# Attention over 32 inducing points and a rational feed-forward layer in one kernel: activation tables swapped per eight units instead of ten, the second layer's matmuls split around the first layer's

## The chip, the cores and the metric

The kernel runs on one core of a Trainium2 chip. The metric is device time in microseconds (us) from start to end of one execution; the time of the kernel before is the median of three runs. Engines are named as in the profile: PE (TensorE matmuls), PEld (its weight loads), DVE (VectorE), ACT (ScalarE), POOL (GpSimd) and SP, which issues the DMAs. Each engine works through its own queue in order, so an instruction that waits holds up everything behind it on that engine.

## The reference

Inputs are x (4 batches of 12480 tokens, 128 channels), 32 inducing rows, w_in (128 x 2048), w_out (2048 x 128) and six scalars a and b. x and the inducing rows are float32, w_in and w_out float64, which the kernel turns to float32 on the chip.

```
h    = softmax(inducing @ x.T / sqrt(128)) @ x        # 32 rows per batch
attn = softmax(x @ h.T / sqrt(128)) @ h               # 12480 rows per batch
h    = attn @ w_in                                    # 49920 x 2048
P    = a0 + a1 h + a2 h^2 + a3 h^3
Q    = 1 + |b0| |h| + |b1| h^2
out  = (P / (Q + 1e-6)) @ w_out                       # 49920 x 128
```

## The kernel before

Since attn is a weighted sum of 32 rows, the kernel multiplies these 32 rows by w_in once per batch (`piece`, tile `st`) and makes each hidden value from 32 softmax weights (tile `at`). Both are kept as high and low f16 parts, stacked on the partitions.

The work of the feed-forward layer is cut into 832 **units** (`main`, line 1044): 4 batches x 26 blocks of 480 tokens x 8 eighths of the hidden layer. A unit has 256 hidden columns, as two halves k = 0, 1 of 128 x 480 values. Its number within its block is q = 0..7. A unit passes through these steps, each on tiles of 960 columns:

- `first` (PE): two f16 matmuls into the PSUM tile `hp`, of which there are three.
- the absolute value u. Units with q = 0, 2, 4, 5, 6 get it as a bit mask on DVE (`mask`), followed by two more matmuls that add a constant to `hp` (`moved`, rows "hp<-same,by"); units with q = 1, 3, 7 have that constant in `st` and get it by an Abs on ACT.
- a product on DVE, `last.g` (rows "l<-u,all,hp"), after which `hp` is free.
- on ACT, for the pair of two units at once (1920 columns), Ln in place of u (rows "u<-u") and later Sigmoid in place of that (rows "u<-u,all"). Ln and Sigmoid lie in different activation tables, so the kernel gathers several pairs of one kind before it turns to the other.
- a second product: for even units on DVE (rows "l<-l,all,u"), for odd units on POOL in two instructions (`last_on_pool`, rows "u<-l,all" and "l<-u").
- `second` (PE): for each half k an f32 matmul by `w_out` into the PSUM tile `po` (there is one), accumulated over the eight units of a block. Each f32 matmul shows as two MATMUL rows, so a unit has four. After q = 7 two more matmuls (rows "po<-at,st") add a linear part. Then `fetch` copies `po` to `oT` on DVE (row "oT<-po") and issues the DMA of the block on SP.

`fast_ticks` (line 885) writes the order out by hand, tick by tick; the order on every engine is fixed to program order. In tick t the mask or Abs is that of unit t, the matmuls of `first` are those of unit t+1, `last.g` is that of unit t-1, the second product is that of units t-13 (DVE) and t-12 (POOL), in odd ticks, and `second` is that of unit t-14, called `done`. A tick whose `done` has q = 0 is `late`: there `second` comes after everything else of the tick, since it needs `po` empty.

Besides, `side` (line 782), called near the end of each tick, makes the attention of the coming blocks and batches in small steps, under a budget of DVE, POOL and PE time per tick. It begins with `self.fetch()`, ahead of its own steps. `second` sets `self.full` after q = 7; `fetch` does nothing while that is None and sets it back to None.

The softmax Exps of the attention wait in a list and are run by `run_act` once per group, in the tick with `turn == TURNS`, right before that group's first Sigmoid. They have a table load of their own.

With TURNS = 5, a group is ten units. Counted from the first unit of the group, the five Lns come in ticks 7 to 11, the five Sigmoids in ticks 12 to 16, and the DVE products in ticks 13, 15, 17, 19, 21.

Of the kernel before, what the change touches and what calls it, by code (L numbers as in the profile page):

```python
# [28 lines left out]
S16 = 2.0 ** 6  # L29
Z = A16 * S16  # L30
LIMIT = 900.0
TURNS = 5
BEHIND = 2 * TURNS + 3


def convert_weights(nc, pool, raw, dst, width, name, rooms):
# [156 lines left out]
class Kernel:  # L193
# [350 lines left out]
    def plain(self, t):  # L544
        return t if self.fast else t.bitcast(F32)
# [302 lines left out]
        for k in range(2):  # L848
            self.nc.tensor.matmul(u.h[:, k], self.by, self.same, start=False, stop=True, skip_group_check=True)

    def second(self, u):

        nc = self.nc
        b, n, q = u.key
        if q == 0:
            self.po = self.ps_o.tile([P, 512], F32, tag="po", name=f"po{u.i}")
        for k in range(2):
            fc = 2 * q + k
            nc.tensor.matmul(self.po[:, 0:BT], self.w_out[:, fc, :], u.g[:, k], start=(fc == 0), stop=(fc == self.NF - 1 and not self.fast))
        if q == self.NP - 1 and self.fast:  # L860
            self.until(lambda: "linear" in self.ready_cols[b])
            for i in range(2):
                nc.tensor.matmul(self.po[:, 0:BT], self.lin[b][:, C * i:C * i + C], u.rhs, start=False, stop=(i == 1))
        if q == self.NP - 1:
            self.full = b, n, self.po
            self.ended = b * self.NB + n + 1
            if n == self.NB - 1:
                self.left = b
# [16 lines left out]
    def fast_ticks(self, units):  # L885

        V, A, p = self.nc.vector, self.nc.scalar, self.params  # L890
        n = len(units)
        at = lambda t: units[t] if 0 <= t < n else None
        plain = lambda u: not self.shifted(u.key[2])

        def mask(u):
            V.tensor_scalar(out=u.u.bitcast(I32), in0=u.h.bitcast(I32), scalar1=0x7FFFFFFF, scalar2=None, op0=ALU.bitwise_and)

        self.first(units[0])
        for t in range(n + BEHIND + 2):
            u, last, d, done = at(t), at(t - 1), at(t - BEHIND), at(t - BEHIND - 1)  # L900
            group, turn = divmod(t - TURNS - 2, 2 * TURNS)
            w = at(2 * TURNS * group + 2 * (turn % TURNS))
            late = done and done.key[2] == 0
            if late:
                self.fetched = self.fetch()
            if t % 2 and at(t + 1):
                self.first(at(t + 1))
            if done and not late:
                self.second(done)
            if t % 2 == 0 and at(t + 1):  # L910
                self.first(at(t + 1))
            if u:
                if t % 2 == 0:
                    u.pair = self.mp.tile([P, 2, 2, BT], F32, tag="u", name=f"u{u.i}", bufs=self.rooms["u"])
                    u.u = u.pair[:, 0]
                    mask(u)
                else:
                    u.u = last.pair[:, 1]
                    if not plain(u):
                        A.activation(u.u, u.h, AF.Abs, bias=p.z_back, scale=1.0)  # L920
            if t % 2 and d:
                V.scalar_tensor_tensor(out=d.g, in0=d.g, scalar=p.z_k3, in1=d.u, op0=ALU.add, op1=ALU.mult)
                self.last_on_pool(at(t - BEHIND + 1), d)
            if u and t % 2 and plain(u):
                mask(u)
            if last:
                last.g = self.new(last, "l")
                V.scalar_tensor_tensor(out=last.g, in0=last.u, scalar=p.z_k1, in1=last.h, op0=ALU.add, op1=ALU.mult)
            if u and plain(u):
                self.moved(u)  # L930
            self.run_act(turn == TURNS)
            if w and turn < TURNS:
                A.activation(w.pair, w.pair, AF.Ln, bias=LAM, scale=LAM / Z)
            elif w:
                A.activation(w.pair, w.pair, AF.Sigmoid, bias=p.lnc, scale=-2.0)
            self.side(u or units[-1])
            if late:
                self.second(done)
        self.fetch()

# [155 lines left out]
```

## Time and profile before

| | us |
|---|---|
| median of 3 runs | 2682.53 (2680.53 to 2683.49) |
| the profiled execution | 2690.05 |
| its span, first to last instruction | 2688.2 |
| PE busy | 2408.0 (90%) |
| DVE busy | 2265.7 (84%) |
| ACT busy | 2099.1 (78%) |
| POOL busy | 1446.9 (54%) |

The first 115 us or so prepare weights and the first batch; the units' last `last.g` is on DVE at 2649 us, and the rest is the way out of the pipeline. Up to about 2100 us the attention's steps run beside the units, after that few are left. Engine names at the front of a row say who worked or waited; "<-" inside names reads "written from"; a bracket or a last column gives idle time ahead of the instruction and who ended it.

### The profile page before, as it was taken

How to read it: one execution, taken by the hardware profiler on the slowest of the kernel's cores; microseconds unless marked ns; L12 is line 12 of the kernel's file. 1: busy time of each engine (PE TensorE's matmuls, PEld its weight loads, DVE VectorE, ACT ScalarE, POOL GpSimd, SP SyncE). 2: the span in 40 equal slices, each digit the busy share in tenths (PEclk: the TensorE clock that was granted, in tenths of full speed). 3: DMA queues.
4: the chain of work that ended last, by engine and by line, in shares of the span. 5: the costliest groups of instructions: out<-in, count | busy, mean ns of one | idle time of the engine just before them, and what ended most of it. 6: DMA issues, size and time to landing. Idle time of an engine off the chain costs nothing.

```text
span 2688.2 us, 25782 instructions
## 1 busy us (share of the span) xinstructions
PE 2408.0 (90%) x8662; PEld 1217.6 (45%) x8662; DVE 2265.7 (84%) x2487; ACT 2099.1 (78%) x1445; POOL 1446.9 (54%) x997
## 2 busy tenths in 40 slices
PE   8589988999988988999999889999989899989997
PEld 5344544554534444554544334545444444444443
DVE  2687888879887997889888788889889899999995
ACT  1167788778777798888777788788878889889886
POOL 0234555555554555556555555556556565666566
PEclk8589999999999999999999999999999999999999
DMA  9112200220112200210212101211010100000000
GB/s 249 42 52 78 73 27 11 59 64 28 48 56 64 65 26 22 63 56 27 58 59 66 44 15 33 63 41 37 25 38 22 41 16 29 17 17 19 15 15 16
DMA packets 117111, 121.02 MB, mean 45 GB/s; under 512 B 13289, under 2 KB 115561, under 8 KB 116969
## 3 DMA queue, kind: packets, MB, share of 16 engines
q1 hardware_dynamic: 116969, 119.28, 15.6%
q8 instruction: 70, 1.15, 0.2%
q14 instruction: 72, 0.59, 0.1%
HBM read 80.89 MB, written 25.56 MB: 40 GB/s over the span
## 4 chain that ended last, share of the span: by engine, by line
PE 45%; DVE 25%; ACT 13%; issue 10%; POOL 2%; DMA 2%; SPq 1%; DVEq 0%; ACTq 0%; POOLq 0%
PE po L177 27%; DVE l L177 11%; DVE u L177 10%; PE hp L177 10%; ACT u L177 9%; ACT L177 3%; PE pd L177 3%; PE ph L177 2%; PE pc L177 1%; DVE oT L177 1%; DVE asm L177 1%; SPq L177 1%; POOL l L177 1%; PE pl L177 1%; POOL u L177 1%
## 5 line engine op out<-in xcount | busy, mean ns | idle before, releaser
L177 PE MATMUL po<-l,w_out 128*128 128x480 f32 x3328 | 1488.9, 581 | 25.8 <-DVE l L177 20.2
L177 DVE SCALAR_TENSOR_TENSOR l<-u,all,hp 128x960 f32<-128x960 f32 x832 | 1001.2, 1204 | 57.4 <-PE hp L177 57.2
L177 POOL TENSOR_SCALAR u<-l,all 128x960 f32<-128x960 f32 x416 | 446.4, 1073 | 1039.4 <-DVE l L177 934.4
L177 POOL TENSOR_TENSOR l<-u 128x960 f32<-128x960 f32 x416 | 928.3, 2231 | 34.6
L177 PEld LDWEIGHTS po<-l,w_out 128*128 128x128 f32 x3328 | 636.2, 194 | 581.0 <-issue 463.2
L177 ACT ACTIVATE u<-u,all 128x1920 f32<-128x1920 f32 x416 | 765.4, 1887 | 1.0
L177 ACT ACTIVATE u<-u 128x1920 f32<-128x1920 f32 x416 | 727.8, 1795 | 17.5 <-DVE l L177 16.5
L177 DVE TENSOR_SCALAR u<-hp 128x960 int32<-128x960 int32 x520 | 596.0, 1146 | 82.2 <-PE hp L177 77.1
L177 ACT ACTIVATE u<-hp,all 128x960 f32<-128x960 f32 x312 | 329.3, 1055 | 426.6 <-PE hp L177 407.5
L177 DVE SCALAR_TENSOR_TENSOR l<-l,all,u 128x960 f32<-128x960 f32 x416 | 519.0, 1248 | 129.8 <-ACT u L177 129.7
L177 PE MATMUL hp<-at,st 128*128 128x480 f16 x1664 | 483.4, 373 | 40.5 <-DVE l L177 36.4
L177 PE MATMUL hp<-same,by 96*128 96x480 f16 x1040 | 303.0, 373 | 146.9 <-DVE u L177 141.6
L177 PEld LDWEIGHTS <-st 128*128 128x128 f16 x1872 | 182.0, 100 | 419.8 <-issue 358.5
L177 ACT ACT_TABLE_LOAD x193 | 247.6, 1283 | 3.9 <-PEq L1089 0.7
L177 PEld LDWEIGHTS <-by 96*128 96x128 f16 x1040 | 102.5, 99 | 280.6 <-issue 181.7
L177 PEld LDWEIGHTS pd<-HT,xTb 128*120 128x120 f32 x832 | 103.0, 197 | 23.3 <-DMA xTb<-x_c 10.0
L177 DVE COPY oT<-po 128x480 f32<-128x480 f32 x104 | 67.7, 651 | 51.0 <-PE po L177 50.7
L177 PE MATMUL pd<-HT,xTb 128*120 128x32 f32 x832 | 100.1, 275 | 9.9 <-DMA xTb<-x_c 9.4
L177 PE MATMUL pc<-xTa,ind 128*128 128x480 f32 x156 | 74.1, 578 | 11.6 <-DMA xTa<-x_c 11.6
L177 PE MATMUL ph<-x,eT 120*32 120x129 f32 x624 | 78.2, 277 | 2.2 <-DMA x<-x_t 2.2
L177 PEld LDWEIGHTS ph<-x,eT 120*32 120x32 f32 x624 | 65.8, 111 | 23.7 <-issue 15.9
L177 PE MATMUL po<-at,st 128*128 128x480 f16 x208 | 59.1, 366 | 0.0
(108 smaller groups left out, 673.4 us busy)
## 6 DMA issues: line engine op xcount, KB each, us to landing
xTb<-x_c SPq DMA_DIRECT2D x104, 240.0 KB, 2.8
out<-oT SPq DMA_DIRECT2D x104, 240.0 KB, 2.0
xTa<-x_c SPq DMA_DIRECT2D x78, 240.0 KB, 2.8
x<-x_t SPq DMA_DIRECT2D x78, 240.0 KB, 3.3
at<-hl SPq DMA_DIRECT2D x416, 30.0 KB, 1.8
xw<-x_t SPq DMA_DIRECT2D x8, 720.0 KB, 14.8
xTw<-x_c SPq DMA_DIRECT2D x5, 960.0 KB, 10.1
raw<-w_in SPq DMA_DIRECT2D x4, 480.0 KB, 13.3
```

Source lines behind the costliest of these rows:

```text
L177: ins = call(*args, **kw)
```

## The change

Three things change in `fast_ticks` and `second`.

First, TURNS is 4 and BEHIND, which was 2 x TURNS + 3 = 13, is written as 13. A group is eight units: counted from its first unit, Lns in ticks 6 to 9, Sigmoids in ticks 10 to 13, DVE products in ticks 13, 15, 17, 19. The distance from a unit's mask to its second product stays 13 ticks. There are 104 groups instead of 84.

Second, in ticks that are not late PE's order is: half k = 0 of `second`, then `first` of unit t+1, then half k = 1 (with the linear part if q = 7). Before, `first` was ahead of both halves in odd ticks and behind both in even ticks.

Third, the call of `fetch` at the start of a late tick is put behind the mask of that tick, and where no unit is left, ahead of `second`.

```
-TURNS = 5
-BEHIND = 2 * TURNS + 3
+TURNS = 4
+BEHIND = 13
...
-    def second(self, u):
+    def second(self, u, ks=(0, 1)):
...
-        if q == 0:
+        if q == 0 and 0 in ks:
             self.po = self.ps_o.tile([P, 512], F32, tag="po", name=f"po{u.i}")
-        for k in range(2):
+        for k in ks:
...
+        if 1 not in ks:
+            return
...
-            if late:
-                self.fetched = self.fetch()
-            if t % 2 and at(t + 1):
+            if done and not late:
+                self.second(done, (0,))
+            if at(t + 1):
                 self.first(at(t + 1))
             if done and not late:
-                self.second(done)
-            if t % 2 == 0 and at(t + 1):
-                self.first(at(t + 1))
+                self.second(done, (1,))
             if u:
                 if t % 2 == 0:
...
                     mask(u)
+                    if late:
+                        self.fetched = self.fetch()
...
             self.side(u or units[-1])
             if late:
+                if not u:
+                    self.fetch()
                 self.second(done)
```

## Rows read from the trace of the kernel before

**Rows 1.** The page's chain of work that ended last, by engine.

```profile
PE 45%; DVE 25%; ACT 13%; issue 10%; POOL 2%; DMA 2%; SPq 1%; DVEq 0%; ACTq 0%; POOLq 0%
```

**Rows 2.** Busy time of each engine in two stretches: a middle one, with attention beside the units, and the last one before the pipeline empties. Columns: stretch, length, busy us (instructions) of PE, PEld, DVE, ACT, POOL, then the granted clock, DMA share, GB/s.

```profile
700.00:1200.00 500.00, 456.72 (x1681) 231.92 (x1680) 426.42 (x447) 402.39 (x279) 270.90 (x194) 0.98 0.17 50
2300.00:2650.00 350.00, 316.42 (x990) 146.03 (x989) 327.45 (x305) 317.00 (x212) 217.33 (x134) 0.99 0.05 17
```

**Rows 3.** Who waited for whom over the whole span: us in total, times, longest us.

```profile
ACT u L177 <- PE hp L177: 407.5, 179, 12.5
PE hp L177 <- DVE u L177: 141.6, 118, 4.0
DVE l L177 <- ACT u L177: 129.7, 64, 5.0
...
DVE oT L177 <- PE po L177: 50.7, 37, 12.2
...
PE hp L177 <- DVE l L177: 36.4, 68, 4.2
...
PE po L177 <- POOL l L177: 4.7, 4, 2.4
```

**Rows 4.** Groups of instructions over the whole span: count, then busy us and mean ns of one, then idle time of the engine ahead of them and who ended it. The first is the DVE product after the sigmoid, then the table loads, the two steps of the POOL product, and two steps of the attention on POOL.

```profile
L177 DVE SCALAR_TENSOR_TENSOR l<-l,all,u 128x960 f32<-128x960 f32 x416 | 519.0, 1248 | 129.8 <-ACT u L177 129.7
...
L177 ACT ACT_TABLE_LOAD x193 | 247.6, 1283 | 3.9 <-PEq L1089 0.7
...
L177 POOL TENSOR_SCALAR u<-l,all 128x960 f32<-128x960 f32 x416 | 446.4, 1073 | 1039.4 <-DVE l L177 934.4 <-PE hp L177 56.3 <-ACT u L177 25.7
L177 POOL TENSOR_TENSOR l<-u 128x960 f32<-128x960 f32 x416 | 928.3, 2231 | 34.6
L177 POOL TENSOR_TENSOR a<-a,asm 120x512 f32<-120x512 f32 (+1 forms) x27 | 28.4, 1052 | 2.4 <-DVE asm L177 2.4
L177 POOL TENSOR_TENSOR st<-gs,st 64x512 f16<-64x512 f32 x16 | 21.3, 1330 | 16.1 <-ACT st L177 9.9 <-DVE st L177 5.3
```

**Rows 5.** The same view from 200 to 2300 us and then from 2300 to 2650 us: the product `last.g`, of which there is one in each tick.

```profile
L177 DVE SCALAR_TENSOR_TENSOR l<-u,all,hp 128x960 f32<-128x960 f32 x674 | 811.4, 1204 | 54.7 <-PE hp L177 54.5
...
L177 DVE SCALAR_TENSOR_TENSOR l<-u,all,hp 128x960 f32<-128x960 f32 x132 | 158.6, 1202 | 2.4 <-PE hp L177 2.4
```

**Rows 6.** ACT in order of time around the change from Ln to Sigmoid in a group with an Exp of the attention: start us, duration us, what, count, and idle time before it.

```profile
1520.56 1.06 ACT L177 ACTIVATE u<-hp,all 128x960 f32<-128x960 f32 x1 [3.14 <-PE hp L177]
1521.52 1.80 ACT L177 ACTIVATE u<-u 128x1920 f32<-128x1920 f32 x1
1523.34 1.28 ACT L177 ACT_TABLE_LOAD   x1
1524.63 1.09 ACT L177 ACTIVATE e<-e,nmc 128x960 f32<-128x960 f32 x1
1525.75 1.28 ACT L177 ACT_TABLE_LOAD   x1
1527.04 1.90 ACT L177 ACTIVATE u<-u,all 128x1920 f32<-128x1920 f32 x1
1528.84 1.04 ACT L177 ACTIVATE u<-hp,all 128x960 f32<-128x960 f32 x1
```

**Rows 7.** DVE at the same place.

```profile
1523.11 1.20 DVE L177 SCALAR_TENSOR_TENSOR l<-u,all,hp 128x960 f32<-128x960 f32 x1
1528.97 1.22 DVE L177 SCALAR_TENSOR_TENSOR l<-l,all,u 128x960 f32<-128x960 f32 x1 [4.66 <-ACT u L177]
...
1532.30 1.20 DVE L177 SCALAR_TENSOR_TENSOR l<-u,all,hp 128x960 f32<-128x960 f32 x1
```

**Rows 8.** PE at the same place.

```profile
1530.24 1.88 PE L177 MATMUL po<-l,w_out 128*128 128x480 f32 x4 [2.92 <-DVE l L177]
...
1533.55 0.56 PE L177 MATMUL hp<-at,st 128*128 128x480 f16 x2 [0.56 <-DVE l L177]
```

**Rows 9.** PE around such a change in a group without an Exp, to the end of its late tick. Rows of `first` (hp<-at,st), `second` (po<-l,w_out) and `moved` (hp<-same,by); the duration of a merged row goes from its first start to its last end.

```profile
2383.28 0.57 PE L177 MATMUL hp<-at,st 128*128 128x480 f16 x2
2383.69 3.38 PE L177 MATMUL po<-l,w_out 128*128 128x480 f32 x8
2386.91 0.57 PE L177 MATMUL hp<-at,st 128*128 128x480 f16 x2
...
2391.47 0.56 PE L177 MATMUL hp<-same,by 96*128 96x480 f16 x2 [1.16 <-DVE u L177]
2392.59 0.57 PE L177 MATMUL hp<-at,st 128*128 128x480 f16 x2 [0.56 <-DVE l L177]
2394.22 0.56 PE L177 MATMUL hp<-same,by 96*128 96x480 f16 x2 [1.06 <-DVE u L177]
```

**Rows 10.** DVE at the same place: the product that waited for the sigmoid.

```profile
2389.13 1.22 DVE L177 SCALAR_TENSOR_TENSOR l<-l,all,u 128x960 f32<-128x960 f32 x1 [2.14 <-ACT u L177]
```

**Rows 11.** DVE at the end of a block: `last.g`, the copy of `po`, a step of the attention, the mask of the late tick.

```profile
998.26 1.21 DVE L177 SCALAR_TENSOR_TENSOR l<-u,all,hp 128x960 f32<-128x960 f32 x1
1000.99 0.66 DVE L177 COPY oT<-po 128x480 f32<-128x480 f32 x1 [1.52 <-PE po L177]
1001.57 0.68 DVE L177 TENSOR_REDUCE amx<-pd 120x16 f32<-120x512 f32 x1
1002.16 1.15 DVE L177 TENSOR_SCALAR u<-hp 128x960 int32<-128x960 int32 x1
```

## The prediction

> **What bounds the kernel now.** I read the chain first: PE holds 45% of it, DVE 25%, ACT 13% [rows 1], so no engine alone sets the time; they hand the path to each other. The stretches say where. In the middle PE is busy 456.72 of 500 us, DVE 426.42 and ACT 402.39; in the last stretch DVE leads with 327.45 of 350, with ACT at 317.00 close behind [rows 2]. The granted clock is 0.98 and 0.99 there, so the clock has nothing to give. A tick (one `last.g` each) lasts 2100/674 = 3.12 us up to 2300 us and 350/132 = 2.65 us after [rows 5]. What a change of order can win is therefore PE's idle time in the middle, and DVE's at the end.
>
> The waits name it [rows 3]. PE waits 141.6 us for masks ahead of `moved` and 36.4 for `last.g` ahead of `first`; DVE waits 129.7 us, 64 times, for a sigmoid. All of this last sum stands before one instruction, the DVE product [rows 4]. It arises at the turn from Ln to Sigmoid: the first Sigmoid is issued one tick before its product, and ACT must first load a table. With an Exp of the attention in between there are two loads: Ln ends, load 1.28, Exp 1.09, load 1.28, Sigmoid 1.90 [rows 6], and DVE stands still for 4.66 us [rows 7].
>
> **Part 1, groups of eight, product three ticks behind the sigmoid.** The product stays 13 ticks behind its mask, so no buffer is held longer. The first Sigmoid moves from tick 12 to tick 10 of its group, the product stays in tick 13. That is two ticks more, 6.2 us (5.3 at the end); the longest of the 64 waits is 5.0 [rows 3]. So I take all 129.7 us off DVE at this place.
>
> How much of that is time? In the group with the Exp, 4.66 us on DVE gave 2.92 + 0.56 = 3.48 us on PE [rows 7, 8], a share of 0.75. In the group without, 2.14 us on DVE gave PE 1.16 + 0.56 = 1.72 us [rows 9, 10], 0.80. Counting only PE's first wait the shares are 0.63 and 0.54. PE had queued work for the rest. I take 0.7, which makes 91 us; the ends are 0.54 (70 us) and 1.0 (130 us), the latter if DVE were the bound throughout, as it is in the last stretch.
>
> It adds table loads. Before there are 84 groups with two, 168; of the 193 [rows 4] one is at the start, so 24 come from Exps. After there are 208 + some 24, 40 more. From a load's start to the next instruction's is 1.29 us [rows 6], so 52 us more on ACT. They are hidden as long as ACT waits for PE: 407.5 us of that now [rows 3].
>
> The page "ScalarE: Activation LUTs" of the Trainium skill speaks against this part: its section on table sets says to gather calls by set, and its section "What ACT_TABLE_LOAD costs" gives 1283 ns for a load and about 1380 ns for a drain, 2.66 us for a switch. The trace agrees on the load and shows no drain: the Ln started at 1521.52 for 1.80 us, and the load begins at 1523.34 [rows 6]. By the page's sum the 40 switches would put 106 us on ACT instead of 52, still less than ACT's waiting time.
>
> What is late next where an Exp runs is the Abs behind the first Sigmoid. In the sample it ends at 1528.84 + 1.04 = 1529.88 [rows 6]. Without the wait DVE would be free at 1523.11 + 1.20 = 1524.31, and the `last.g` that reads this Abs comes 1532.30 - 1528.97 = 3.33 us after the product's start [rows 7], at 1527.64. So 2.2 of the 4.66 us would come back there. After the change the group's start falls on the same q each time (ten units drift against the block of eight, eight don't), and it is this one: Sigmoid in a tick of q = 2, Abs of q = 3 next. Part 2 eases it by 0.8 to 1.6 us (below). I take 1.0 us x 24 Exps x 0.7 = 17 us; the ends are 0 and 2.2 x 24 = 53.
>
> **Part 2, halves around `first`.** The work is the same. Eight rows of `second` take 2386.91 - 2383.69 = 3.22 us, 0.40 each, and the pair of `first` ahead of them 0.41, with no gap at either join [rows 9]. So the additional changes between f16 and f32 matmuls cost nothing, and a half lasts 0.80 us.
>
> In even ticks `first` moves 0.80 us forward: the Abs that waits for it (3.14 us in [rows 6]) starts earlier. In odd ticks it moves 0.80 us back, and has those 0.80 us of work ahead of it while it waits for `hp`; this removes some of the 36.4 us [rows 3], but not that of late ticks, which keep their order: I take 10 us, bounds 0 and 30. Against it, the mask of each even unit is the first thing DVE does in its tick, and can start up to 0.80 us later; `last.g`, products and the copy are queued behind it, and PE's `moved` waits for that. DVE mostly catches up, since PE then has a half, a `first` and more ahead of its next `moved`. But DVE waits for `po` before its copy only 37 times in 104 blocks [rows 3], so in most blocks it is the later one, and some of the delay reaches PE: I take 0.2 us a block, 20 us, bounds 0 and 0.80 x 104 = 83.
>
> One wait is added: in odd ticks `first` stands behind a half that needs POOL's product. That takes 1.07 + 2.23 = 3.3 us after DVE's product [rows 4], and PE wants it two ticks, 6.2 us, after the tick began, 5 us after DVE's 1.25. Only the 27 + 16 steps of the attention on POOL (1.05 and 1.33 us [rows 4]) come near; PE waits 4.7 us for POOL in all today [rows 3]. I take 0; the bound is 43 x 0.4 = 17 us.
>
> **Part 3, the copy behind the mask, does nothing.** `second` sets `self.full` in the tick of q = 7, before that tick calls `side`, and `side` begins with `fetch`. The late tick's own call, one tick on, finds None, in either place; so do the new calls. The trace bears it out: the copy stands directly behind `last.g`, and a step of the attention, issued by `side` after its `fetch`, follows it ahead of the mask [rows 11]. A copy made at the start of the late tick would stand behind that step. So the copy, its DMA on SP and the wait of the late tick stay: PE's 1.06 us ahead of `moved` after the copy [rows 9], about 100 us over 104 blocks, the largest part of the 141.6.
>
> **The sum**, against the profiled execution's 2690.05 us (span 2688.2, so 1.85 outside it): -91 + 17 - 10 + 20 + 0 = -64, thus 2626. That execution is 7.5 us over the median of the runs, 2682.53; on that scale the forecast is **2619 us**.
>
> **Rivals.**
>
> *ACT takes over.* ACT gets 52 us more, at fixed places, two loads in each eight ticks. If the Abs behind them is late, DVE waits there. For it: ACT is at 317.00 of 350 us at the end, and its 132 ticks there get 132 x (2/8 - 2/10) x 1.29 = 8.5 us of loads more, up to 325.5, level with DVE's 327.45 [rows 2, 5]. Against it: in the middle 98 of 500 us are free. Price: the 17 us become 53, and of the gain's end stretch some 8 are lost: 2619 + 36 + 8 = 2663. Here the skill's rule above would count more, its drain if it appeared.
>
> *The halves cost more than the sigmoids give (the slower side).* Place: the mask of an even unit, 0.80 us later, with DVE the later one at the copy. If one mask per block passes its delay on in full, that is 83 us instead of 20, and with the Exps' 53 instead of 17 the sum is -91 + 53 - 10 + 83 = +35: 2718. It decides from the point where less than 91 - 53 + 10 = 48 us, 0.46 us a block, is absorbed. The 37 copies that wait speak against it.
>
> *The whole wait is time.* Share 1.0, no Abs behind it, halves without loss: -130 - 10 = -140, 2543; half way to it is 2580.
>
> *I misread the third part.* If the copy did move behind the mask, up to its 0.6 us would leave PE's wait in 104 blocks: 62 us less, 2557.
>
> **How the numbers follow.** Forecast (2590 to 2645) 0.63; ACT takes over (2645 to 2680) 0.16; halves, slower, 0.09; whole wait or nearly (2543 to 2590) 0.09; third part 0.03. The range takes in the forecast and most of ACT's case and of the large gains: 2572 to 2668. A measurement of this kernel can tell about 0.2% (5 us) from no change. Faster: 0.63 + 0.15 + 0.09 + 0.03, less a little from the edges, 0.88; same 0.04; slower 0.08.
>
> **What would show it.** Right: DVE's wait for ACT ahead of the product falls from 129.7 to below 10 us; about 232 table loads; ACT's wait for PE shrinks; PE's wait of about 1 us ahead of the late tick's `moved` stays, and the copy still stands directly behind `last.g`. Waits of 0.5 to 2 us of `last.g` for ACT, where an Exp runs, are the 17 us. Wrong: such waits in groups without an Exp (ACT's case); DVE's waits for PE ahead of masks well over today's with PE's wait for masks over 160 us (halves); a copy behind the mask.

## The result, and the profile after

The changed kernel takes 2593.70 us (median of 4 runs, 2589.76 to 2599.01) against 2681.53 us before on the same chip: a ratio of 0.9677, 95% interval 0.9653 to 0.9700, 88 us less. The forecast of 2619 us had the sign and the range right and was 25 us short in size. The profiled execution took 2591.88 us, its span is 2589.7 us.

The page of the changed kernel: busy time and share of each engine, and the chain that ended last.

```profile
PE 2376.2 (92%) x8662; PEld 1206.7 (47%) x8662; DVE 2267.1 (88%) x2487; ACT 2151.0 (83%) x1487; POOL 1448.1 (56%) x997
...
PE 50%; DVE 28%; issue 8%; ACT 7%; POOL 2%; DMA 1%; SPq 1%; DVEq 0%; POOLq 0%; ACTq 0%
```

ACT's part of the chain falls from 13% [rows 1] to 7%, though ACT is 52 us busier. PE's idle time, span less busy, falls from 2688.2 - 2408.0 = 280.2 us to 213.5: 66.7 us, near the 64 of the forecast. The rest of the span's 98.5 us, 31.8, is PE *busy* time, with the same 8662 matmul rows. No step of the prediction had that.

Who waited for whom, changed kernel (us in total, times, longest us):

```profile
ACT u L177 <- PE hp L177: 289.1, 157, 9.2
...
PE hp L177 <- DVE u L177: 124.6, 123, 3.2
DVE u L177 <- PE hp L177: 118.3, 124, 5.8
...
DVE oT L177 <- PE po L177: 68.4, 37, 11.1
...
PE hp L177 <- DVE l L177: 17.9, 29, 4.6
DVE l L177 <- ACT u L177: 16.5, 10, 2.4
...
PE po L177 <- POOL l L177: 8.4, 13, 1.9
```

And three of its groups of instructions:

```profile
L177 DVE SCALAR_TENSOR_TENSOR l<-u,all,hp 128x960 f32<-128x960 f32 x832 | 1001.8, 1204 | 44.8 <-PE hp L177 29.9 <-ACT u L177 14.0
...
L177 DVE SCALAR_TENSOR_TENSOR l<-l,all,u 128x960 f32<-128x960 f32 x416 | 523.9, 1260 | 2.4 <-ACT u L177 2.4
...
L177 ACT ACT_TABLE_LOAD x235 | 301.5, 1283 | 4.7 <-PEq L1093 0.7
```

Beside [rows 3, 4]: the product's wait for the sigmoid is 2.4 us instead of 129.7; 14.0 us of it are back as waits of `last.g` for an Abs; there are 42 more table loads, and ACT's own wait for PE has shrunk by 118 us. PE's wait for masks is still there, and DVE's wait for PE ahead of masks has risen to 118.3 us from 77.1 in the same view before:

```profile
DVE u L177 <- PE hp L177: 77.1, 56, 3.7
```

Where the 14.0 us are, ACT and then DVE around an Exp of the attention, changed kernel:

```profile
439.39 1.80 ACT L177 ACTIVATE u<-u 128x1920 f32<-128x1920 f32 x1
441.20 1.28 ACT L177 ACT_TABLE_LOAD   x1
442.50 1.09 ACT L177 ACTIVATE e<-e,nmc 128x960 f32<-128x960 f32 x1
443.60 1.28 ACT L177 ACT_TABLE_LOAD   x1
444.89 1.90 ACT L177 ACTIVATE u<-u,all 128x1920 f32<-128x1920 f32 x1
446.69 1.04 ACT L177 ACTIVATE u<-hp,all 128x960 f32<-128x960 f32 x1
```

```profile
442.40 1.33 DVE L177 SCALAR_TENSOR_TENSOR l<-l,all,u 128x960 f32<-128x960 f32 x1
443.66 1.20 DVE L177 SCALAR_TENSOR_TENSOR l<-u,all,hp 128x960 f32<-128x960 f32 x1
444.79 1.14 DVE L177 TENSOR_SCALAR u<-hp 128x960 int32<-128x960 int32 x1
447.77 1.21 DVE L177 SCALAR_TENSOR_TENSOR l<-u,all,hp 128x960 f32<-128x960 f32 x1 [1.84 <-ACT u L177]
```

ACT does what it did in [rows 6]. DVE's product runs at 442.40, while ACT is still loading tables; it reads a sigmoid of the group before. What waits is the `last.g` that reads the Abs behind the first Sigmoid, for 1.84 us: the Abs ends at 447.73.

The end of a block, DVE and then PE, changed kernel:

```profile
2366.79 1.20 DVE L177 SCALAR_TENSOR_TENSOR l<-u,all,hp 128x960 f32<-128x960 f32 x1
2367.92 0.65 DVE L177 COPY oT<-po 128x480 f32<-128x480 f32 x1
2368.48 1.14 DVE L177 TENSOR_SCALAR u<-hp 128x960 int32<-128x960 int32 x1
```

```profile
2368.05 0.56 PE L177 MATMUL hp<-at,st 128*128 128x480 f16 x2
2369.68 0.56 PE L177 MATMUL hp<-same,by 96*128 96x480 f16 x2 [1.07 <-DVE u L177]
```

The copy still stands between `last.g` and the mask, and PE still waits 1.07 us for that mask, as in [rows 9].

### The profile page after: what moved, and what is told of

Its sections match the earlier page's. It is cut to its first block, busy times and chain, and to the rows that moved or that the text cites. A ratio compares the mean times of both kernels' runs of the same rounds, so it can differ in the third digit from the quotient of the medians.

```text
span 2589.7 us, 25944 instructions
## 1 busy us (share of the span) xinstructions
PE 2376.2 (92%) x8662; PEld 1206.7 (47%) x8662; DVE 2267.1 (88%) x2487; ACT 2151.0 (83%) x1487; POOL 1448.1 (56%) x997
## 4 chain that ended last, share of the span: by engine, by line
PE 50%; DVE 28%; issue 8%; ACT 7%; POOL 2%; DMA 1%; SPq 1%; DVEq 0%; POOLq 0%; ACTq 0%
PE po L177 29%; DVE l L177 12%; DVE u L177 11%; PE hp L177 11%; ACT u L177 5%; PE pd L177 3%; PE ph L177 3%; PE pc L177 2%; DVE oT L177 1%; ACT L177 1%; POOL l L177 1%; DVE asm L177 1%; POOL u L177 1%; SPq L177 1%; PE pl L177 1%
## 5 line engine op out<-in xcount | busy, mean ns | idle before, releaser
L177 PE MATMUL po<-l,w_out 128*128 128x480 f32 x3328 | 1568.2, 575 | 10.6 <-POOL l L177 8.4
L177 PEld LDWEIGHTS po<-l,w_out 128*128 128x128 f32 x3328 | 624.3, 192 | 372.3 <-issue 209.2
L177 ACT ACTIVATE u<-u 128x1920 f32<-128x1920 f32 x416 | 737.5, 1797 | 3.0 <-DVE l L177 1.8
L177 DVE TENSOR_SCALAR u<-hp 128x960 int32<-128x960 int32 x520 | 597.2, 1148 | 125.1 <-PE hp L177 118.3
L177 ACT ACTIVATE u<-hp,all 128x960 f32<-128x960 f32 x312 | 328.2, 1052 | 289.8 <-PE hp L177 289.1
L177 PE MATMUL hp<-at,st 128*128 128x480 f16 x1664 | 477.5, 369 | 20.4 <-DVE l L177 17.9
L177 PE MATMUL hp<-same,by 96*128 96x480 f16 x1040 | 301.3, 371 | 129.9 <-DVE u L177 124.6
L177 ACT ACT_TABLE_LOAD x235 | 301.5, 1283 | 4.7 <-PEq L1093 0.7
L177 DVE COPY oT<-po 128x480 f32<-128x480 f32 x104 | 67.8, 652 | 68.9 <-PE po L177 68.4
```

The costliest lines, as they stand in the source:

```text
L177: ins = call(*args, **kw)
```

## The experiments

Two theories. **A**: the time came from the distance between sigmoid and product; the halves are a small loss beside it; the third part does nothing. **B**: the halves carry a good part of the gain, or the shorter, aligned group does, whatever the distance. Ratios are to the kernel before on the same chip, with 95% intervals.

| kernel | us | ratio | interval |
|---|---|---|---|
| the change | 2593.70 | 0.9677 | 0.9653 to 0.9700 |
| groups of eight alone | 2576.01 | 0.9615 | 0.9594 to 0.9636 |
| halves alone | 2652.16 | 0.9894 | 0.9876 to 0.9912 |
| the change, copy really behind the mask | 2561.36 | 0.9561 | 0.9543 to 0.9578 |
| the change, product 11 ticks behind the mask | 2648.93 | 0.9890 | 0.9873 to 0.9907 |
| groups of ten, product 15 ticks behind | 3168.77 | 1.1816 | 1.1796 to 1.1837 |
| the change, halves in even ticks alone | 2573.62 | 0.9586 | 0.9568 to 0.9605 |
| the change, halves in odd ticks alone | 2601.15 | 0.9707 | 0.9693 to 0.9720 |
| groups of eight, old order, copy behind the mask | 2556.26 | 0.9533 | 0.9519 to 0.9547 |
| the change with a table load more per group | 2610.93 | 0.9744 | 0.9731 to 0.9758 |
| before, PE's stall filled | 2695.01 | 1.0056 | 1.0042 to 1.0071 |
| groups of eight, halves in even ticks, copy behind the mask | 2545.07 | 0.9500 | 0.9484 to 0.9516 |
| the same, Exps ahead of the Lns | 2531.20 | 0.9445 | 0.9429 to 0.9461 |

**Each part alone.** The kernel before with the groups alone:

```
-TURNS = 5
-BEHIND = 2 * TURNS + 3
+TURNS = 4
+BEHIND = 13
```

> The kernel before with groups of eight and the product three ticks behind the sigmoid, PE's old order and nothing else. If the removed wait for the sigmoid is nearly the whole gain and the halves are about neutral, 2594 to 2615 us (ratio to before 0.967 to 0.975), with DVE's wait ahead of the product below 10 us. If the halves bring a third of the gain themselves, 2620 to 2635 us (0.977 to 0.983). In both cases last.g waits longer for an Abs where an Exp runs than with the halves: 25 to 50 us in all against 14.

Measured 2576.01 us, 102 us less than before, below both expectations: the groups alone are faster than the whole change. The busy times of its page, and its waits:

```profile
PE 2359.7 (92%) x8662; PEld 1207.4 (47%) x8662; DVE 2266.3 (88%) x2487; ACT 2149.0 (83%) x1487; POOL 1448.8 (56%) x997
...
PE hp L177 <- DVE u L177: 118.0, 113, 3.3
DVE u L177 <- PE hp L177: 69.8, 54, 5.0
...
DVE l L177 <- ACT u L177: 23.9, 14, 3.4
```

Of the 23.9 us, 3.4 stand ahead of the product, and 20.5 are `last.g` waiting for an Abs, less than the 25 to 50 expected.

The halves alone are the changed kernel with the old constants:

```
-TURNS = 4
+TURNS = 5
 BEHIND = 13
```

> The kernel before with the halves alone: groups of ten, product one tick behind the sigmoid. As predicted in the sum (10 us won, 20 lost), 2685 to 2700 us (1.001 to 1.007). If the halves bring a part of the gain, 2650 to 2668 us (0.988 to 0.995). If they help only where the sigmoid's wait is gone, 2677 to 2686 us (0.998 to 1.002) here and more in the whole change than in the groups alone.

Measured 2652.16 us, 26 us less than before, inside the second expectation. DVE's wait for ACT fell too, to 85.9 us (54 times) from 129.7, and ACT's wait for PE to 373.7 from 407.5. By the order of the code the reason is that `first` comes 0.80 us earlier in even ticks, so that ACT's Abs, Lns and the Sigmoid behind them start earlier; no run sets that apart in groups of ten. So the halves win part of the same wait; the two gains, 102 and 26, do not add, and together they give 88.

**The halves taken apart.** One kernel splits `second` in even ticks alone, the other in odd ticks alone; the other ticks have their order of before.

```
+            split = t % 2 == 0
-            if done and not late:
+            if done and not late and split:
                 self.second(done, (0,))
+            if done and not late and not split and t % 2 == 0:
+                self.second(done)
             if at(t + 1):
                 self.first(at(t + 1))
-            if done and not late:
+            if done and not late and split:
                 self.second(done, (1,))
+            if done and not late and not split and t % 2:
+                self.second(done)
```

The second has `t % 2 == 1` in the first line.

> The changed kernel with halves in even ticks alone; odd ticks have first ahead of second, as before the change. If the halves cost by the even units' masks that come 0.80 us later in odd ticks, and give by the Abs that starts earlier in even ones, this is no slower than the groups alone: 2562 to 2578 us (0.957 to 0.963), DVE's wait for PE ahead of masks near 70 us, last.g's wait for an Abs near 14. If splitting itself costs, 2582 to 2590 us (0.964 to 0.967).

> The changed kernel with halves in odd ticks alone; even ticks have second ahead of first, as before the change. If the cost lies in the masks of even units, all of it is here: 2592 to 2606 us (0.968 to 0.973), DVE's wait for PE ahead of masks near 118 us, last.g's wait for an Abs 20 us or more. If splitting itself costs, 2582 to 2590 us (0.964 to 0.967).

Measured 0.9586 and 0.9707, each in its first range. Against the groups alone (0.9615) the odd ticks' halves cost 0.9%, and the even ticks' are no loss and perhaps a small gain (the intervals overlap). The wait of DVE for PE ahead of masks, in the first and in the second:

```profile
DVE u L177 <- PE hp L177: 58.6, 49, 4.2
...
DVE u L177 <- PE hp L177: 137.0, 133, 5.8
```

Added up from the timelines, the masks of even units have about 53 us of this wait in the groups alone, 54 with the even ticks' halves, 125 with the odd ticks' and 116 in the change. So the loss comes with what the prediction named, the even unit's mask that comes 0.80 us later, and splitting as such costs nothing that shows.

**Distance or group.** The change with the product one tick behind the sigmoid again, in groups of eight:

```
 TURNS = 4
-BEHIND = 13
+BEHIND = 11
```

> The changed kernel with the product 11 ticks behind the mask, so one tick behind the first sigmoid again, with groups of eight and halves as in the change. If the distance is what counts, the wait comes back in 104 groups instead of 84, 1.2 to 1.6 us each: 125 to 165 us on DVE, 85 to 115 us of time, 2680 to 2710 us (1.000 to 1.011). If the group's length or its fixed place against the block counts, 2594 to 2615 us (0.967 to 0.975).

Measured 2648.93 us, 55 us more than the change and between the two expectations. DVE's wait for ACT is back:

```profile
DVE l L177 <- ACT u L177: 121.5, 82, 4.1
```

So the distance is most of it; the 1.1% that is left against before is what the halves alone give (0.9894), which this kernel has too. With the product one tick behind the sigmoid, the shorter, aligned group by itself wins nothing that shows. Then the distance without the shorter group, the kernel before with

```
-BEHIND = 2 * TURNS + 3
+BEHIND = 2 * TURNS + 5
```

> The kernel before with the product 15 ticks behind the mask instead of 13, so three ticks behind the first sigmoid, with groups of ten and 193 table loads. If the distance alone carries the gain, 2570 to 2590 us (0.960 to 0.967), the wait for the sigmoid below 10 us. If holding the pairs two ticks longer makes masks wait for a buffer that POOL still reads, that wait shows as DVE's wait for POOL, 0.3 us or more in each even tick (over 120 us), and the time is 2630 us or more (0.982 and up).

Measured 3168.77 us, the second expectation's case at far more than its size. The product's wait for the sigmoid is gone in its trace, idle 0.0 us ahead of it, and masks wait instead. The groups, then DVE and POOL in order of time:

```profile
L177 DVE TENSOR_SCALAR u<-hp 128x960 int32<-128x960 int32 x520 | 600.0, 1154 | 579.9 <-POOL l L177 517.4 <-POOL x L177 37.5 <-PE hp L177 20.9
L177 DVE SCALAR_TENSOR_TENSOR l<-l,all,u 128x960 f32<-128x960 f32 x416 | 506.1, 1217 | 0.0
```

```profile
1000.18 1.21 DVE L177 SCALAR_TENSOR_TENSOR l<-l,all,u 128x960 f32<-128x960 f32 x1
1001.41 1.22 DVE L177 SCALAR_TENSOR_TENSOR l<-u,all,hp 128x960 f32<-128x960 f32 x1
1004.97 1.16 DVE L177 TENSOR_SCALAR u<-hp 128x960 int32<-128x960 int32 x1 [2.34 <-POOL l L177]
```

```profile
1001.57 1.07 POOL L177 TENSOR_SCALAR u<-l,all 128x960 f32<-128x960 f32 x1 [3.62 <-DVE l L177]
1002.72 2.22 POOL L177 TENSOR_TENSOR l<-u 128x960 f32<-128x960 f32 x1
```

The eight pair tiles hold 16 units. At 15 ticks the new pair's mask comes in the tick after POOL began with the last product that reads the old pair, and starts 0.03 us after that product ends (1002.72 + 2.22 = 1004.94). So with these eight tiles a longer distance is paid for in masks, and the distance had to come from a shorter group; groups of ten with more tiles were not tried.

**The copy really behind the mask.** In the changed kernel `side` is kept from fetching in the fast path, so the late tick's own call does it:

```
-        if self.fetch() or self.fetched:
+        if (not self.fast and self.fetch()) or self.fetched:
```

> The changed kernel with the third part made to work: side no longer fetches, so the copy is made by the late tick's own call behind its mask. If PE's wait ahead of the late tick's moved is on the path, it falls by the copy's 0.57 to 0.66 us in most of 104 blocks, 40 to 60 us: 2535 to 2555 us (0.945 to 0.953). If last.g behind the copy, or second of the next block, which needs po empty, takes its place, 2580 to 2597 us (0.962 to 0.969).

Measured 0.9561, 32 us less than the change and between the expectations. DVE and PE at the end of a block there:

```profile
1007.39 1.15 DVE L177 TENSOR_SCALAR u<-hp 128x960 int32<-128x960 int32 x1
1008.46 0.65 DVE L177 COPY oT<-po 128x480 f32<-128x480 f32 x1
```

```profile
1008.59 0.56 PE L177 MATMUL hp<-same,by 96*128 96x480 f16 x2 [0.50 <-DVE u L177]
```

Its waits:

```profile
PE hp L177 <- DVE u L177: 68.4, 93, 2.9
...
DVE oT L177 <- PE po L177: 19.2, 5, 11.1
```

The sample's wait is 0.50 us instead of 1.07, and PE's wait for masks 68.4 us in all instead of 124.6. DVE's own wait for `po` ahead of the copy falls as well, from 68.4 to 19.2 us, since the mask no longer stands behind it. The third part's place in the code was worth about 32 us; as written its calls find nothing to copy. By the code the same holds for the kernel before with the third part alone, which was not run.

The same with the old order of PE, that is the groups alone with the third part and this line:

> Groups of eight with PE's old order (as in the run of the groups alone, ratio 0.9615) and the copy made behind the late tick's mask. If the copy's gain does not depend on the halves, 28 to 34 us from 2576: 2542 to 2550 us (0.949 to 0.953), with PE's wait for masks near 70 us as in the run of the copy. If old order gives the time back at first or second behind it, 2565 to 2577 us (0.958 to 0.963).

Measured 0.9533, just above the first range: about 22 us beside the groups' 0.9615. That it is less than the 32 beside the halves is not clear of the intervals.

**The price of table loads.** The changed kernel with a short Exp ahead of each group's first Sigmoid:

```
             self.run_act(turn == TURNS)
+            if w and turn == TURNS:
+                A.activation(self.spin, self.ceps, AF.Exp, bias=0.0, scale=1.0)
...
```

> The changed kernel with an Exp of one column (128x1) ahead of the first Sigmoid of every group, so that the groups without an Exp of the attention load a table more: some 80 loads of 1.29 us and as many short Exps, 120 us more on ACT (2151 to 2270 us). If table loads are hidden in ACT's waits for PE, only the Abs behind the Sigmoid comes a little late: 2594 to 2622 us (0.967 to 0.978), and ACT's wait for PE falls by 80 us or more from 289. If loads stand on the path, 2690 us or more (1.003 and up).

Measured 2610.93 us, 17 us more than the change. Its groups:

```profile
L177 ACT ACT_TABLE_LOAD x311 | 399.0, 1283 | 4.9 <-PEq L1096 0.7
...
L177 ACT ACTIVATE spin<-ceps 128x1 f32<-128x1 f32 x104 | 20.7, 199 | 0.8
```

ACT is 110 us busier than in the change (2261.4 against 2151.0), and 85 us of that came out of its wait for PE (289.1 to 204.1). The waits of `last.g` for an Abs rise from 14.0 to 36.3 us, about the price. The 42 loads of the change are half as much work; in proportion they would cost some 8 us, an estimate from this run's 17.

**The stall filled.** To ask what a stalled PE loses beyond the wait, the kernel before repeats `first` of the coming unit ten matmuls long where an Exp precedes the Sigmoid; the repeats write the same values.

```
...
             if t % 2 == 0 and at(t + 1):
                 self.first(at(t + 1))
+            if turn == TURNS + 1 and self.exped and at(t + 1):
+                self.refill(at(t + 1))
...
```

> The kernel before, where after an Exp of the attention PE repeats the ten matmuls of first of the coming unit (the same values once more, 2.0 us) in the tick of the product that waits for the sigmoid, so that PE idles less while DVE waits as long as before. If a part of the sigmoid's price is TensorE's clock, which the trace shows at 0.5 after such stalls (109 us in all from 200 to 2540 us, 41 in the changed kernel), half clock falls to 60 to 85 us and the time to 2660 to 2673 us (0.992 to 0.997). If the clock is no part of it, the repeats are hidden or cost: 2680 to 2700 us (1.000 to 1.008).

Measured 2695.01 us. DVE's wait for ACT stayed at 131.7 us, but stretches at half of the full clock, told of at the end, stayed too (106 us from 200 to 2540 us, against 109), so the filling did not do what it was for. The run shows that 250 matmuls more cost 15 us here, and leaves open what part of the price was the clock.

**What won, together.** Groups of eight, halves in even ticks, the copy behind the mask:

> Groups of eight, halves in even ticks alone, the copy made behind the late tick's mask: the three parts that each won. If they add, 20 to 31 us from 2574: 2543 to 2555 us (0.948 to 0.953). If the even ticks' halves win nothing beside the moved copy, 2555 to 2565 us (0.953 to 0.957).

Measured 0.9500, in the first range, and then the Exps ahead of the group's first Ln:

```
-            self.run_act(turn == TURNS)
+            self.run_act(turn == 0)
```

> The fastest run so far (groups of eight, halves in even ticks, copy behind the mask, ratio 0.950) with the attention's Exps run ahead of a group's first Ln instead of between its last Ln and its first Sigmoid. If the Abs behind the first Sigmoid is what the Exps delay, last.g's wait for it falls from 20 us to below 6 and the time by 5 to 15 us: 2530 to 2542 us (0.944 to 0.949). If the delay only moves to the Abs behind the first Ln, or is hidden anyway, 2542 to 2552 us (0.949 to 0.953).

Measured 0.9445, 2531.20 us, at the lower edge. The group of `last.g` in the kernel without and with this last edit:

```profile
L177 DVE SCALAR_TENSOR_TENSOR l<-u,all,hp 128x960 f32<-128x960 f32 x832 | 1002.5, 1205 | 81.3 <-PE hp L177 60.2 <-ACT u L177 19.7
```

```profile
L177 DVE SCALAR_TENSOR_TENSOR l<-u,all,hp 128x960 f32<-128x960 f32 x832 | 1001.4, 1204 | 71.6 <-PE hp L177 61.5 <-ACT u L177 8.2
```

The wait for an Abs falls from 19.7 to 8.2 us, not below the 6 expected, which shows that the Exps made most of it. The time falls by 0.55%, about 15 us, give or take 6 by the two intervals, so the 11.5 us of the wait fit.

## Why the prediction was right, and by how much it was short

*The sigmoid's wait.* That all of the 129.7 us would leave the product held (2.4). What it is worth in time was too small: -91 us by the share of 0.7, -74 with the Abs behind it; the groups alone gave -102. They took DVE's wait for ACT from 129.7 to 23.9 us, so 105.8 us of wait went with 102 us of time. The mis-sized term is this share, and behind it the sentence that "the clock has nothing to give". The share was read from PE's idle time, and there it was not too small: in the groups alone that falls to 2574.2 - 2359.7 = 214.5 us, by 65.7, where 74 was forecast. Beside it PE's busy time falls by 48.3 us, which the sum had nowhere. I had read the granted clock as a mean over long stretches, 0.98 and 0.99 [rows 2]. Per execution it is 0.961 in the profile of before and 0.960 to 0.965 in eleven runs of it, 0.971 to 0.974 in the four of the change, and 0.975 to 0.978 in the five of the groups alone. The share of the clock that was not granted is (1 - 0.961) x 2688.2 = 105 us before and (1 - 0.974) x 2589.7 = 67 us after. That difference, 38 us, is of the size of the 31.8 us of busy time that PE lost. Nearly half of the 105 us lies in the first 200 us, where the granted clock is 0.76 before and 0.78 after; the difference comes almost all from the half-clock stretches behind them (last section), 109 us before and 41 after; half of such a stretch is lost, so that is 34 us less. The forecast's -64 was PE's idle time alone, and that fell by 66.7. That these two are so near is partly luck: the groups took off 8 us less idle time than forecast, and the halves added none where 10 was. The clock's part is read from the traces; the one run that was to set it apart did not.

*The Abs behind the Sigmoid.* Right in its place, somewhat too large: 1.0 us x 24 on DVE was expected, 14.0 us in 9 waits is what the trace shows, and moving the Exps took more than half of such waits away.

*Table loads.* 235 against the 232 forecast. The 1283 ns of the Trainium skill ("ScalarE: Activation LUTs", section "What ACT_TABLE_LOAD costs") are what the rows have; its drain of 1380 ns does not show after either: the Exp starts 1.30 us after its load did (441.20 to 442.50). The rule of the Trainium skill (same page, section "Table sets: the hidden batching unit") to gather calls by set would have kept the group of ten; here most of the loads' time was hidden and the wait was not.

*Halves.* -10 + 20 = +10 us was expected. Beside the groups they cost 0.6%, 17 us; that the late masks of even units go with it is what the split by parity shows. The path to PE was not as forecast: PE's wait for masks rises only from 118.0 to 124.6 us, its idle time not at all (214.5 and 213.5), and the 17 us stand as busy time of PE (2359.7 and 2376.2). Why its rows last longer there stays open. The prediction's turning point has a slip: the sum comes out slower when the halves cost over 48 us, so when less than 35 of the 83 is absorbed. That they would win if the sigmoid's wait stayed (0.9894 alone) I had not worked out: I priced the earlier Abs only behind an Exp.

*Third part.* It does nothing, as read from the code and [rows 11]. Made to work it gives about 32 us, where the rival had 62. PE's wait for masks did fall by 56.2 us, but not all of that was time: PE's idle time fell by 38.9 us in all (213.5 to 174.6), so other waits took its place, and its busy time rose by 11.3 (2376.2 to 2387.5).

*POOL's half.* Taken at 0; PE's wait for POOL went from 4.7 to 8.4 us.

*The rivals.* ACT did not take over: it is 83% busy, and even 110 us more cost 17. The slower side, halves that eat the gain, had the right masks and a fifth of the price. The rival by which the whole wait is time was nearest for the first part, as its 105.8 and 102 us show; in the whole change the Abs and the halves took part of it back.

## What to carry to other kernels

Where an engine waits at the turn between two batches of another engine's work, give the consumer more ticks behind the producer; if the buffers are full, a smaller batch gives these ticks at the same depth, and here the additional switches cost little, as that engine waited for others anyway. Take an edit of several parts alone, part by part: here one part was worth more alone than all three, one half of another was the loss, and the third needed one line elsewhere to do anything. When a flag says "nothing to do" at the new place of a call, look for the other caller that got there first.

## What the runs showed of the hardware that I had not expected

After a stall TensorE ran on at half clock here. The kernel before, in a group with an Exp: stretches of its trace (columns as in [rows 2]; the clock is the first number after the engines'), then PE in order of time.

```profile
2130.00:2137.00 7.00, 5.21 (x16) 2.10 (x14) 2.38 (x4) 6.94 (x6) 2.30 (x2) 1.00 0.00 0
2137.00:2143.40 6.40, 2.81 (x8) 1.16 (x9) 6.33 (x7) 6.40 (x5) 4.33 (x3) 0.99 0.00 0
2143.40:2146.80 3.40, 2.93 (x6) 1.44 (x5) 3.40 (x4) 1.46 (x1) 1.54 (x2) 0.52 0.00 0
2146.80:2150.00 3.20, 2.20 (x10) 0.89 (x9) 2.55 (x4) 1.18 (x2) 1.74 (x1) 1.00 0.17 61
```

```profile
2138.08 1.88 PE L177 MATMUL po<-l,w_out 128*128 128x480 f32 x4 [2.87 <-DVE l L177]
2139.80 0.57 PE L177 MATMUL hp<-at,st 128*128 128x480 f16 x2
2142.88 0.65 PE L177 MATMUL hp<-same,by 96*128 96x480 f16 x2 [2.52 <-DVE u L177]
2143.99 0.96 PE L177 MATMUL hp<-at,st 128*128 128x480 f16 x2 [0.47 <-DVE l L177]
2144.74 2.72 PE L177 MATMUL po<-l,w_out 128*128 128x480 f32 x4
```

PE waited 2.87 and 2.52 us; the granted clock then fell from 1.00 to 0.52, near the lower of its two levels (1.2 of 2.4 GHz), and four rows of `second` took 2.72 us, where the four at 2138.08 took 1.88 and [rows 9] has eight in 3.38. By the trace's clock records such stretches sum to 109 us between 200 and 2540 us before and to 41 us after. So in this kernel a wait on the path was paid for twice, once as idle time and once in the work behind it; a mean clock of 0.98 hides that.
